# Three-layer attention and expert kernel: the first layer's maxima and subtractions taken head by head, constants and one weight load moved

## Chip, cores, metric

One core of a Trainium2 chip runs the whole kernel. The metric is the device time of the launch in microseconds (us), the median of several runs. The profiled execution is one further run whose trace was recorded.

## What is computed

The input is a batch of B = 4 sequences of S = 576 positions with 8 heads of 64 columns. Three layers follow each other; the change is in the first, a linear attention:

```python
def phi(x):
    proj = np.einsum('bhsd,df->bhsf', x, w_phi)               # 64 -> 128 features
    proj = proj - np.max(np.abs(proj), axis=-1, keepdims=True)
    return np.concatenate([np.exp(proj), np.exp(-proj)], axis=-1)
q_p, k_p = phi(q), phi(k)
kv  = np.einsum('bhsf,bhsd->bhfd', k_p, v)
z   = np.sum(k_p, axis=2)
num = np.einsum('bhsf,bhfd->bhsd', q_p, kv)
den = np.einsum('bhsf,bhf->bhs', q_p, z)[..., None] + 1e-06
x   = num / den
```

The second layer sends each position through causal attention of 2 of 4 experts, chosen by a gate on x. The third sends each position through one of 8 two-layer networks (512 to 1024 to 512 columns), with a choice that can stick to that of the position before.

## The kernel before

The first layer works on 16 units, one for each sequence and pair of heads (`PhaseA`). `raw` holds k and q of the two heads, head 0 in partitions 0 to 63 and head 1 in 64 to 127. `proj` (L221) is called three times for a unit: for k (`nm` "k", 4 tiles of 128 positions), for the last 64 positions of k and q together ("e", one tile) and for q ("q", 4 tiles). Each call multiplies by `w_phi` (L237) into one PSUM tile for each head (`pjk_0` and `pjk_1`, or `pje`, `pjq`). VectorE then takes for each head the largest absolute value of each position (L241: `mxk`, `mxe`, `mxq`) and subtracts it (L242: `uk`, `ue`, `uq`).

- `feat_k` (L245): ScalarE takes exp of +u and of -u (L251 for 512 positions of both heads in one instruction, L252 for the last 64) into the one buffer `kp`; GpSimd adds up the four tiles (L255 to L257) into `zs`.
- `feat_q` (L259): TensorE transposes `uq` of a head (L268, tile `tr`), ScalarE takes its two exps (L270, `qp`).
- `kv` (L279) multiplies v by kp into the PSUM tile `Y`; `keys` (L288) adds the column sums, and ScalarE copies Y out (L291, tile `kvt`).
- `kvtrans` (L301, L306): TensorE transposes the last columns of q (from `ue`) and the unit before's `kvt` into one PSUM tile, also called `kvt`; ScalarE copies it (L307, `kvs`).
- `num` (L323, copied into x by VectorE at L326 for one half and by ScalarE at L328 for the other) and `den` (L340, `dn` at L342, stored to DRAM as `dd` at L344) end a unit.

The order of one round is a string of step names: the projections of unit i are laid between the transpositions of unit i-1 and the products of units i-1 and i-2:

```python
A_STEPS = ("k0 e0 q0 t f0 x0 t f1 t a kv0 kv1 A t kv2 kv3 t n0 n1 z0 a t t A s0 d0 d1 t")
```

PSUM has 5 banks for the tiles `pjk`, `pjq`, `tr` and `kvt` together, given out in turn; `pje` and the tiles of `num`, `den` and the gates share two others. So the bank that a step takes in a round is fixed by how many were taken before it: in most rounds the tile of `kvtrans` (step x0) takes the bank that `pjk_0` of the same round held, and the second `tr` (step f1) that of `pjk_1`. Either can be written as soon as VectorE has subtracted that head.

A tile framework turns this into each engine's final order: it puts instructions in an order of its own, and `issue_after(ins)` tells it to issue what is recorded inside after `ins`. Before the change only the background work uses that (`Background.step`, L95; an instruction recorded with `anchor` is what it is issued after). This background work, the gate of a finished sequence, the load of the experts' weights (`wr_s`, L1099, by registers that are read from `ri_b`, L637 and L638) and their splitting in two (L1116 on ScalarE, L1117 on VectorE), runs at the steps named "t" in the later rounds. After the first two sequences are done (rounds 9 to 11) the most of it comes together with the units' own work.

`make_consts` (L143) sets up identities, a mask and a few small tables (`iota`, `lower`, `ones`) with some eight short VectorE instructions (L152 to L174, and L1011 elsewhere). `load` (L203) issues the loads of `raw`, by SyncE; for the first unit in three pieces, with the load of `w_phi` (L211) behind the first.

Of the kernel before, what the change touches and what calls it, by code (L numbers as in the profile page):

```python
# [12 lines left out]
AF = mybir.ActivationFunctionType  # L13
OP = mybir.AluOpType
AX = mybir.AxisListType
# [5 lines left out]
NF = 128  # L21
# [36 lines left out]
def rd(ap):  # L58
    return ap.bitcast(F32)
# [8 lines left out]
class Background:  # L68
# [3 lines left out]
    def __init__(self, tc):  # L72
        self.q, self.tc, self.anchors, self.now = [], tc, {}, 0

    def add(self, name, gen, held=True, lane="", after=(), at=None, wait=0, rate=1):
        e = dict(name=name, gen=gen, held=held, lane=lane, after=after, wake=self.now + wait, rate=rate)
        self.q.insert(len(self.q) if at is None else at, e)
# [67 lines left out]
def make_consts(ctx, tc, E1=4, E2=8):  # L145
    nc = tc.nc
    cp = ctx.enter_context(tc.tile_pool(name="consts", bufs=1))
    k = Consts()
    one = cp.tile([128, 128], F32, name="ones")
    make_identity(nc, one)  # L150
    eye = cp.tile([128, 128], F32R, name="ident")
    nc.vector.tensor_copy(eye, one)  # L152
    k.ident = rd(eye)
    k.identb = cp.tile([128, 128], BF16, name="identb")
    nc.vector.tensor_copy(k.identb, k.ident)
    k.mask = cp.tile([128, 128], BF16, name="cmask")
    nc.vector.memset(k.mask, 0.0)
    nc.gpsimd.affine_select(out=k.mask, in_=k.mask, pattern=[[-1, 128]], base=0, channel_multiplier=1,
                            compare_op=OP.is_ge, fill=-1e30)

    k.identr = eye[:, 0:64]
    k.maskr = cp.tile([128, 64], F32R, name="cmaskr")
    nc.vector.tensor_copy(k.maskr, k.mask[:, 0:64])
    k.ones = one
    nc.vector.memset(k.ones, 1.0)
    ii = cp.tile([128, 8], I32, name="iota_i")
    nc.gpsimd.iota(ii, pattern=[[1, 8]], base=0, channel_multiplier=0)
    k.iota = cp.tile([128, 8], F32, name="iota")
    nc.vector.tensor_copy(k.iota, ii)
    k.iota1 = cp.tile([128, 8], F32, name="iota1")  # L170
    nc.vector.tensor_scalar(k.iota1, k.iota, 1.0, None, op0=OP.add)

    k.lower = cp.tile([128, 4, 4], F32, name="lower")
    nc.vector.tensor_tensor(k.lower, k.iota[:, None, 0:4].to_broadcast([128, 4, 4]),  # L174
                            k.iota[:, 0:4, None].to_broadcast([128, 4, 4]), op=OP.is_lt)
    return k


class PhaseA:


    def __init__(self, ctx, tc, k, ps, gk, dr, hl, kq, v, w_phi, x1_tile, bg):
        nc = tc.nc
        self.gk, self.dr, self.hl = gk, dr, hl
        self.nc, self.k, self.kq, self.v, self.bg, self.x1_tile = nc, k, kq, v, bg, x1_tile
        self.p2 = ctx.enter_context(tc.tile_pool(name="a_2", bufs=2))
        self.p3 = ctx.enter_context(tc.tile_pool(name="a_3", bufs=2))
        self.p1 = ctx.enter_context(tc.tile_pool(name="a_1", bufs=2))
        self.ps = ps
        self.w_phi = self.p3.tile([128, NF], F32, name="a_w", bufs=1)  # L190
        self.w_in = w_phi
        self.vts = []
        for i in range(3):
            vt = self.p3.tile([128, QT, 2, 64], F32, name=f"a_v{i}", bufs=1)
            nc.gpsimd.memset(vt[64:128, 4], 0.0)
            self.vts.append(vt)

        self.kp = self.p3.tile([128, QT, 2, 256], F32, name="a_kp", bufs=1)
        nc.gpsimd.memset(self.kp[64:128, 4], 0.0)
        self.st = {}  # L200
        self.units = [(b, p) for b in range(B) for p in range(NP)]

    def load(self, i):  # L203

        nc, (b, p) = self.nc, self.units[i]
        raw = self.p2.tile([128, 2 * S], F32, tag="raw", name=f"raw_{i}", bufs=3)
        self.st[i] = {"raw": raw}
        for c in (slice(0, 256), slice(256, 640), slice(640, 2 * S)) if i == 0 else (slice(0, 640), slice(640, 2 * S)):
            nc.sync.dma_start(raw[:, c], self.kq[b, p, :, c])
            if i == 0 and c.start == 0:  # L210
                nc.sync.dma_start(self.w_phi, self.w_in)  # L211

    def load_v(self, i):
        nc, (b, p), r = self.nc, self.units[i], self.st[i]
# [6 lines left out]
    def proj(self, i, nm):  # L221


        nc, r = self.nc, self.st[i]
        w, raws = self.w_phi, r["raw"]
        n = 1 if nm == "e" else 4
        u = r["u" + nm] = self.p3.tile([128, n, 256], F32, tag=f"u{nm}", name=f"u{nm}_{i}")
        mx = self.p3.tile([128, 2, n], F32, tag=f"mx{nm}", name=f"mx{nm}_{i}")
        if n == 1:
            pt = [self.ps.tile([128, HALF], F32, tag="mm", name=f"pj{nm}_{i}_{h}") for h in range(2)]  # L230
        else:
            pt = [self.ps.tile([128, 512], F32, tag="X", name=f"pj{nm}_{i}_{h}") for h in range(2)]
        for t in range(n):
            for h in range(2):
                p = slice(64 * h, 64 * h + 64)
                c = dict(k=0, e=512, q=640)[nm] + 128 * t
                nc.tensor.matmul(pt[h][:, 128 * t:128 * t + 128], raws[p, c:c + 128], w[p], start=True, stop=True)  # L237
        for h in range(2):
            src = pt[h][:, 0:128 * n].rearrange("p (t f) -> p t f", f=NF)
            m = mx[:, h]  # L240
            nc.vector.tensor_reduce(m, src, axis=AX.X, op=OP.max, apply_absolute_value=True)  # L241
            self.bg.anchor(nc.vector.tensor_tensor(u[:, :, NF * h:NF * h + NF], src,  # L242
                                                   m[:, :, None].to_broadcast([128, n, NF]), op=OP.subtract))

    def feat_k(self, i):  # L245
        nc, r = self.nc, self.st[i]
        u, e = r["uk"], r["ue"]
        kp = self.kp
        zs = r["zs"] = self.p3.tile([128, 2, 2, 256], F32, tag="zs", name=f"zs_{i}", bufs=1)
        for sg, sc in ((0, 1.0), (1, -1.0)):  # L250
            nc.scalar.activation(kp[:, 0:4, sg, :], u[:, 0:4, :], AF.Exp, scale=sc)  # L251
            self.bg.anchor(nc.scalar.activation(kp[0:64, 4, sg, :], e[0:64, 0, :], AF.Exp, scale=sc))  # L252

            add = nc.gpsimd.tensor_tensor
            add(zs[:, :, sg, :], kp[:, 0:2, sg, :], kp[:, 2:4, sg, :], op=OP.add)  # L255
            add(zs[0:64, 0, sg, :], zs[0:64, 0, sg, :], kp[0:64, 4, sg, :], op=OP.add)
            add(zs[:, 0, sg, :], zs[:, 0, sg, :], zs[:, 1, sg, :], op=OP.add)  # L257
# [88 lines left out]
    def fin(self, b):  # L346
# [20 lines left out]
        for p in range(n):  # L367
            load(p)
        yield 5
        for p in range(NP):  # L370
            (nc.vector if last and p % 2 else nc.gpsimd).tensor_tensor(x1[:, p, :], x1[:, p, :], rbs[p], op=OP.mult)
            if p == 0 and n == 3:
                load(3)
            if not last:
                yield
# [1225 lines left out]
def kern(tc, kq, v, w_phi, b_gate, wqkv, wo, c_gate, w1, w2, out):  # L1601
    nc = tc.nc
    with ExitStack() as ctx:


        def pool(name, c=ctx, **kw):
            return c.enter_context(tc.tile_pool(name=name, bufs=kw.pop("bufs", 2), reuse_waits="tile", **kw))

        k = make_consts(ctx, tc)
        cp = pool("const2", bufs=1)  # L1610
        dr = ctx.enter_context(tc.tile_pool(name="dram", bufs=1, space=DRAM))
# [119 lines left out]
```

## Time and profile before

| | us |
|---|---|
| three runs | 562.77, 560.4, 562.26 |
| their median | 562.26 |
| profiled execution | 560.32 |
| its span in the trace | 558.4 |
| projections of the 16 units, first and last | start 3.2 and about 160 |

The profiled execution is 1.94 us below the median of the runs; 1.92 us of its own time lie outside its span. A page gives busy times and, in the list of costliest groups, what an engine sat idle for. A wait row names an engine and line, what it waited for, the total, the count and the longest. A timeline row gives the start, the busy time of a run of equal instructions, and in brackets the idle time before them; a chain row gives the start and the length of a piece of the chain that ended last. The program has one TensorE that is rarely idle: what matters is where it waits.

### The profile page before, as it was taken

What the parts mean: (1) busy time and instruction counts of PE and PEld (TensorE: products, weight loads), DVE (VectorE), ACT (ScalarE), POOL (GpSimd) and SP (SyncE); (2) the same over time, 40 slices, a digit from 0 to 9 for tenths busy, and PEclk for the clock granted to TensorE, in tenths of its full rate; (3) what the DMA queues carried; (4) which work ended last, traced back from release to release, by engine and by line L of the source; (5) the groups of instructions that cost most, each with busy time, mean ns of one, the idle gap of its engine ahead of it and who ended that gap; (6) DMA issues with size and microseconds to landing.
All of it is one profiled execution on the core that took longest, in us unless ns stands there. A gap on an engine that the chain in (4) does not pass through costs nothing.

```text
span 558.4 us, 11721 instructions
## 1 busy us (share of the span) xinstructions
PE 529.3 (95%) x4456; PEld 440.0 (79%) x4456; DVE 358.7 (64%) x952; ACT 269.5 (48%) x609; POOL 178.1 (32%) x222
## 2 busy tenths in 40 slices
PE   6999999899999999998998999999999999998995
PEld 5666665566667597768776888898999999997995
DVE  5776677986772777968796876842754265617450
ACT  2857465574574366947659653630442145114200
POOL 5563584368437222221103200120405040503000
PEclk9999999999999999999999999999999999999999
DMA  8323263445105222700200510273336133713011
GB/s 245 123 77 117 84 222 105 127 143 168 50 5 174 75 69 87 228 1 2 76 1 1 188 41 2 76 251 100 123 113 194 44 123 115 256 65 124 2 45 47
DMA packets 32708, 57.06 MB, mean 102 GB/s; under 512 B 7012, under 2 KB 17636, under 8 KB 31620
## 3 DMA queue, kind: packets, MB, share of 16 engines
q1 hardware_dynamic: 32644, 56.24, 31.0%
q8 instruction: 37, 0.61, 0.4%
q14 instruction: 27, 0.22, 0.1%
HBM read 41.86 MB, written 14.36 MB: 101 GB/s over the span
## 4 chain that ended last, share of the span: by engine, by line
PE 72%; DVE 14%; ACT 5%; issue 4%; DMA 4%; POOL 0%; SPq 0%; DVEq 0%; ACTq 0%; POOLq 0%
PE Y L279 6%; PE pq_s L702 6%; PE pn L323 5%; PE po_c L63 5%; PE po_c L64 5%; PE po_c L65 5%; PE ph_c L63 4%; PE ph_c L65 4%; PE ph_c L64 4%; PE py_s L848 3%; PE pd L340 3%; PE pjk L237 3%; DVE mxk L241 3%; PE pg L439 2%; PE pt_s L821 2%
## 5 line engine op out<-in xcount | busy, mean ns | idle before, releaser
L63 PE MATMUL ph_c<-xh_c,w1h_c 128*128 128x288 f32 x256 | 76.7, 300 | 0.0
L1415 ACT ACTIVATE h_c<-ph_c 128x288 fp32r<-128x288 f32 x64 | 25.8, 408 | 104.9 <-PE ph_c L65 104.6
L63 PE MATMUL po_c<-h_c,w2h_c 128*128 128x288 f32 x256 | 76.2, 297 | 0.0
L64 PE MATMUL ph_c<-xl_c,w1h_c 128*128 128x288 f32 x256 | 75.7, 296 | 0.0
L65 PE MATMUL ph_c<-xh_c,w1l_c 128*128 128x288 f32 x256 | 75.5, 296 | 0.0
L64 PE MATMUL po_c<-h_c,w2h_c 128*128 128x288 f32 x256 | 75.5, 295 | 0.0
L65 PE MATMUL po_c<-h_c,w2l_c 128*128 128x288 f32 x256 | 75.4, 295 | 0.0
L255 POOL TENSOR_TENSOR zs<-a_kp 128x512 f32<-128x512 f32 x32 | 42.3, 1336 | 68.7 <-PE Y L288 42.3
L270 ACT ACTIVATE qp<-tr 128x512 f32<-128x512 f32 x64 | 35.1, 610 | 50.2 <-PE tr L268 50.2
L1416 DVE SCALAR_TENSOR_TENSOR h_c<-ph_c,h_c 128x288 fp32r<-128x288 f32 x64 | 28.5, 453 | 33.4 <-ACT h_c L1415 33.1
L63 PEld LDWEIGHTS ph_c<-xh_c,w1h_c 128*128 128x128 f32 x256 | 48.1, 188 | 1.8 <-DVE h_c L1416 0.6
L63 PEld LDWEIGHTS po_c<-h_c,w2h_c 128*128 128x128 f32 x256 | 48.1, 188 | 0.9 <-issue 0.9
L65 PEld LDWEIGHTS ph_c<-xh_c,w1l_c 128*128 128x128 f32 x256 | 48.0, 188 | 0.5 <-issue 0.5
L1385 POOL TENSOR_TENSOR xl_c<-x,xh_c 128x576 fp32r<-128x576 f32 x16 | 26.5, 1680 | 68.4 <-ACT xh_c L1384 68.3
L64 PEld LDWEIGHTS ph_c<-xl_c,w1h_c 128*128 128x128 f32 x256 | 48.1, 188 | 0.0
L65 PEld LDWEIGHTS po_c<-h_c,w2l_c 128*128 128x128 f32 x256 | 48.1, 188 | 0.0
L64 PEld LDWEIGHTS po_c<-h_c,w2h_c 128*128 128x128 f32 x256 | 48.1, 188 | 0.0
L702 PE MATMUL pq_s<-xh_b,w_s 128*128 128x288 f32 x192 | 43.6, 305 | 2.7 <-DVE q_s L670 1.7
L1437 DVE TENSOR_TENSOR fo_c<-po_c,pb 128x288 f32<-128x288 f32 x32 | 14.4, 455 | 47.7 <-PE po_c L65 29.6
L279 PE MATMUL Y<-a_kp,a_v 128*64 128x256 f32 x320 | 41.1, 386 | 0.0
L251 ACT ACTIVATE a_kp<-uk 128x1024 f32<-128x1024 f32 x32 | 33.6, 1052 | 13.0 <-DVE uk L242 6.4
L1370 POOL TENSOR_TENSOR w2l_c<-w2raw_c,w2h_c 128x1024 fp32r<-128x1024 f32 x6 | 17.4, 2921 | 65.6 <-ACT w2h_c L1368 65.6
(314 smaller groups left out, 1268.4 us busy)
## 6 DMA issues: line engine op xcount, KB each, us to landing
w1raw_c<-in_w_dram SPq DMA_DIRECT2D x16, 512.0 KB, 4.3
w2raw_c<-in_w_dram SPq DMA_DIRECT2D x16, 512.0 KB, 5.0
raw<-in_kq_dram SPq DMA_DIRECT2D x15, 320.0 KB, 3.1
rb<-d SPq DMA_DIRECT2D x32, 144.0 KB, 3.5
x1d<-x SPq DMA_DIRECT2D x4, 1152.0 KB
x2d<-x SPq DMA_DIRECT2D x4, 1152.0 KB
raw<-in_kq_dram SPq DMA_DIRECT2D x16, 256.0 KB, 3.5
a_v<-in_v_dram SPq DMA_DIRECT2D x16, 256.0 KB, 4.2
```

The lines of the kernel that those rows point to most:

```text
L63: nc.tensor.matmul(out, lh, rh, start=start, stop=False, **kw)
L64: nc.tensor.matmul(out, lh, rl, start=False, stop=False, **kw)
L65: return nc.tensor.matmul(out, ll, rh, start=False, stop=stop, **kw)
L251: nc.scalar.activation(kp[:, 0:4, sg, :], u[:, 0:4, :], AF.Exp, scale=sc)
L255: add(zs[:, :, sg, :], kp[:, 0:2, sg, :], kp[:, 2:4, sg, :], op=OP.add)
L270: self.bg.anchor(nc.scalar.activation(qp[:, h, sg, 0:512], tp, AF.Exp, scale=sc))
L279: nc.tensor.matmul(Y[64 * h:64 * h + 64, 0:256], vt[:, t, h, :], kp[:, t, :, h * NF:(h + 1) * NF], start=t == 0, stop=t == 4)
L323: nc.tensor.matmul(pn[64 * h:64 * h + 64, :], kvs[:, sg, 64 * h:64 * h + 64], qp[:, h, sg, c], start=sg == 0, stop=sg == 1)
L702: self.nc.tensor.matmul(out, self.wqkv[t][:, wj, ch, 0:m], x[:, ch, c], start=wj == ch == 0 and x is xh, stop=wj == 1 and ch == 3)
L1385: self.bg.anchor(nc.gpsimd.tensor_tensor(xl[:, ch], x[:, ch], rd(xh[:, ch]), op=OP.subtract))
L1415: nc.scalar.activation(hh[:, c], ph, AF.Relu),
L1416: nc.vector.scalar_tensor_tensor(hl[:, c], ph, 0.0, rd(hh[:, c]), op0=OP.max, op1=OP.subtract))
```

## The change

In `proj`, each reduction is issued after `self.last`, which is at first the last of the constants (`k.last`, the instruction that makes `lower`) and from then on the latest subtraction of k. In the first unit, ScalarE takes the exps of k head by head (four of 512 columns in place of two of 1024). The load of `w_phi` is issued by ScalarE, no longer by SyncE. In the changed kernel the lines below move by one or by twelve: L241 is L244, L242 is L245, L251 is L263 (in the first unit L260), L268 is L280, L326 is L338.

```diff
--- before.py
+++ after.py
@@ -171,8 +171,8 @@
     nc.vector.tensor_scalar(k.iota1, k.iota, 1.0, None, op0=OP.add)
 
     k.lower = cp.tile([128, 4, 4], F32, name="lower")
-    nc.vector.tensor_tensor(k.lower, k.iota[:, None, 0:4].to_broadcast([128, 4, 4]),
-                            k.iota[:, 0:4, None].to_broadcast([128, 4, 4]), op=OP.is_lt)
+    k.last = nc.vector.tensor_tensor(k.lower, k.iota[:, None, 0:4].to_broadcast([128, 4, 4]),
+                                     k.iota[:, 0:4, None].to_broadcast([128, 4, 4]), op=OP.is_lt)
     return k
 
 
@@ -197,6 +197,7 @@
 
         self.kp = self.p3.tile([128, QT, 2, 256], F32, name="a_kp", bufs=1)
         nc.gpsimd.memset(self.kp[64:128, 4], 0.0)
+        self.last = k.last
         self.st = {}
         self.units = [(b, p) for b in range(B) for p in range(NP)]
 
@@ -208,7 +209,7 @@
         for c in (slice(0, 256), slice(256, 640), slice(640, 2 * S)) if i == 0 else (slice(0, 640), slice(640, 2 * S)):
             nc.sync.dma_start(raw[:, c], self.kq[b, p, :, c])
             if i == 0 and c.start == 0:
-                nc.sync.dma_start(self.w_phi, self.w_in)
+                nc.scalar.dma_start(self.w_phi, self.w_in)
 
     def load_v(self, i):
         nc, (b, p), r = self.nc, self.units[i], self.st[i]
@@ -238,17 +239,28 @@
         for h in range(2):
             src = pt[h][:, 0:128 * n].rearrange("p (t f) -> p t f", f=NF)
             m = mx[:, h]
-            nc.vector.tensor_reduce(m, src, axis=AX.X, op=OP.max, apply_absolute_value=True)
-            self.bg.anchor(nc.vector.tensor_tensor(u[:, :, NF * h:NF * h + NF], src,
-                                                   m[:, :, None].to_broadcast([128, n, NF]), op=OP.subtract))
+            with ExitStack() as c:
+                c.enter_context(self.bg.tc.issue_after(self.last.ins))
+                nc.vector.tensor_reduce(m, src, axis=AX.X, op=OP.max, apply_absolute_value=True)
+            last = nc.vector.tensor_tensor(u[:, :, NF * h:NF * h + NF], src,
+                                           m[:, :, None].to_broadcast([128, n, NF]), op=OP.subtract)
+            if nm == "k":
+                self.last = last
+            self.bg.anchor(last)
 
     def feat_k(self, i):
         nc, r = self.nc, self.st[i]
         u, e = r["uk"], r["ue"]
         kp = self.kp
         zs = r["zs"] = self.p3.tile([128, 2, 2, 256], F32, tag="zs", name=f"zs_{i}", bufs=1)
+        if not i:
+            for h in range(2):
+                for sg, sc in ((0, 1.0), (1, -1.0)):
+                    c = slice(h * NF, (h + 1) * NF)
+                    nc.scalar.activation(kp[:, 0:4, sg, c], u[:, 0:4, c], AF.Exp, scale=sc)
         for sg, sc in ((0, 1.0), (1, -1.0)):
-            nc.scalar.activation(kp[:, 0:4, sg, :], u[:, 0:4, :], AF.Exp, scale=sc)
+            if i:
+                nc.scalar.activation(kp[:, 0:4, sg, :], u[:, 0:4, :], AF.Exp, scale=sc)
             self.bg.anchor(nc.scalar.activation(kp[0:64, 4, sg, :], e[0:64, 0, :], AF.Exp, scale=sc))
 
             add = nc.gpsimd.tensor_tensor
```

VectorE at the start of the program, before, from its third instruction on (uk, ue: the subtracted k and last columns of unit 0; `_0` and `_1` behind pjk and pje are the heads):

```order
L241 TENSOR_REDUCE mxk_159<-pjk_0_160 128x4
L241 TENSOR_REDUCE mxk_159<-pjk_1_161 128x4
L242 TENSOR_TENSOR uk_158<-pjk_0_160,mxk_159 128x4x128
L242 TENSOR_TENSOR uk_158<-pjk_1_161,mxk_159 128x4x128
L169 CAST iota<-iota_i 128x8
L241 TENSOR_REDUCE mxe_175<-pje_0_176 128x1
L152 CAST ident<-ones 128x128
L163 CAST cmaskr<-cmask 128x64
L171 TENSOR_SCALAR iota_79<-iota 128x8
L155 CAST identb<-ident 128x128
L165 MEMSET ones 128x128
L174 TENSOR_TENSOR lower<-iota 128x16
```

And with the change:

```order
L169 CAST iota<-iota_i 128x8
L152 CAST ident<-ones 128x128
L163 CAST cmaskr<-cmask 128x64
L171 TENSOR_SCALAR iota_79<-iota 128x8
L155 CAST identb<-ident 128x128
L165 MEMSET ones 128x128
L174 TENSOR_TENSOR lower<-iota 128x16
L1023 COPY b_ex<-iota 128x8
L244 TENSOR_REDUCE mxk_159<-pjk_0_160 128x4
L245 TENSOR_TENSOR uk_158<-pjk_0_160,mxk_159 128x4x128
L244 TENSOR_REDUCE mxk_159<-pjk_1_161 128x4
L245 TENSOR_TENSOR uk_158<-pjk_1_161,mxk_159 128x4x128
```

The constants now stand in front of the first reduction, and each head of k is reduced and subtracted before the other is begun.

VectorE in unit 3, whose k is `pjk_0_429` and `pjk_1_430` before:

```order
L326 COPY x_0_391<-pn_1_399 128x288
L241 TENSOR_REDUCE mxk_428<-pjk_0_429 128x4
L241 TENSOR_REDUCE mxk_428<-pjk_1_430 128x4
L242 TENSOR_TENSOR uk_427<-pjk_0_429,mxk_428 128x4x128
L242 TENSOR_TENSOR uk_427<-pjk_1_430,mxk_428 128x4x128
L241 TENSOR_REDUCE mxe_444<-pje_0_445 128x1
```

And with the change, where the same tiles are `pjk_0_431` and `pjk_1_432`:

```order
L338 COPY x_0_393<-pn_1_401 128x288
L244 TENSOR_REDUCE mxk_430<-pjk_0_431 128x4
L245 TENSOR_TENSOR uk_429<-pjk_0_431,mxk_430 128x4x128
L244 TENSOR_REDUCE mxk_430<-pjk_1_432 128x4
L245 TENSOR_TENSOR uk_429<-pjk_1_432,mxk_430 128x4x128
L244 TENSOR_REDUCE mxe_446<-pje_0_447 128x1
```

Only the second and third row of k have changed places; it is so in every unit from 3 to 9 and from 12 to 15.

VectorE in round 10, where the second half of the gate of the first two sequences runs (`perm`, `ws`, `ri_b`: the experts chosen; `x_1`: a half of unit 7's result; `dn`: its denominators; `uk_1418`: k of unit 10), before:

```order
L468 TENSOR_REDUCE perm_0_1377<-u_0_1342 128x4
L520 TENSOR_REDUCE ws_1381<-c_0_1379 128x20
L637 CAST ri_b_0_1383<-perm_0_1377 1x1
L637 CAST ri_b_1_1395<-perm_0_1377 1x1
L326 COPY x_1_900<-pn_1_1325 128x288
L342 TENSOR_SCALAR dn_1354<-pd_0_1355 128x288
L342 TENSOR_SCALAR dn_1354<-pd_1_1365 128x288
L241 TENSOR_REDUCE mxk_1419<-pjk_0_1420 128x4
L241 TENSOR_REDUCE mxk_1419<-pjk_1_1421 128x4
L242 TENSOR_TENSOR uk_1418<-pjk_0_1420,mxk_1419 128x4x128
L242 TENSOR_TENSOR uk_1418<-pjk_1_1421,mxk_1419 128x4x128
```

And with the change (the reduction of k's first head, `mxk_1421<-pjk_0_1422`, stands nine rows before the first of these, its subtraction five rows before):

```order
L338 COPY x_1_902<-pn_1_1327 128x288
L472 TENSOR_REDUCE rk_1346<-u_0_1344 128x4
L245 TENSOR_TENSOR uk_1420<-pjk_1_1423,mxk_1421 128x4x128
L475 TENSOR_TENSOR hot_0_1348<-rk_1346,iota 128x16
L354 TENSOR_SCALAR dn_1356<-pd_0_1357 128x288
L478 TENSOR_TENSOR u_0_1344<-hot_0_1348,iota 128x16
L529 TENSOR_TENSOR c_0_1381<-w_0_1213,hot_0_1348 128x80
L480 TENSOR_REDUCE perm_0_1379<-u_0_1344 128x4
L532 TENSOR_REDUCE ws_1383<-c_0_1381 128x20
L354 TENSOR_SCALAR dn_1356<-pd_1_1367 128x288
L649 CAST ri_b_0_1385<-perm_0_1379 1x1
L649 CAST ri_b_1_1397<-perm_0_1379 1x1
```

Unit 10's k, which stood behind the gate and both `dn`, is now mixed with the gate's last steps; the two `ri_b` stood in front of `x_1` and both `dn` and now stand behind them.

SyncE at the same place (`wsd`, `dd`: stores of the gate and of `dn`; `wr_s`: the first weights of the second layer), before:

```order
L1026 DMA wsd<-ws_1381 128x20
L638 TENSOR_LOAD ri_b_0_1383
L638 ISA x2
L638 TENSOR_LOAD ri_b_1_1395
L638 ISA x2
L1099 ISA
L1099 DMA wr_s_1407<-in_wqkv_dram 128x768
L1099 ISA
L1099 DMA wr_s_1407<-in_wqkv_dram 128x768
L344 DMA dd_901<-dn_1354 4x576
```

And with the change:

```order
L1038 DMA wsd<-ws_1383 128x20
L356 DMA dd_903<-dn_1356 4x576
L650 TENSOR_LOAD ri_b_0_1385
L650 ISA x2
L650 TENSOR_LOAD ri_b_1_1397
L650 ISA x2
L1111 ISA
L1111 DMA wr_s_1409<-in_wqkv_dram 128x768
L1111 ISA
L1111 DMA wr_s_1409<-in_wqkv_dram 128x768
```

The store `dd` stood behind the weights and now stands in front of the register loads that the weights' addresses come from.

## Rows read from the trace of the kernel before

**Rows 1.** Part 1 of the page: busy us, share of the span, instructions.
```profile
PE 529.3 (95%) x4456; PEld 440.0 (79%) x4456; DVE 358.7 (64%) x952; ACT 269.5 (48%) x609; POOL 178.1 (32%) x222
```

**Rows 2.** Waits of PE, stretch 0 to 210.
```profile
PE kvt L301 <- DVE uk L242: 4.6, 11, 1.0
...
PE tr L268 <- DVE uk L242: 0.4, 1, 0.4
```

**Rows 3.** Timeline of PE in round 5, 46.7 to 51.3.
```profile
49.95 0.41 PE L301 MATMUL kvt<-ident,ue 128*128 128x128 f32 x2 [0.36 <-DVE uk L242]
...
50.55 0.63 PE L268 MATMUL tr<-ident,uq 128*128 128x128 f32 x4
```

**Rows 4.** Timeline of DVE, the same stretch.
```profile
47.92 1.29 DVE L241 TENSOR_REDUCE mxk<-pjk 128x4 f32<-128x512 f32 x2 [0.97 <-PE pjk L237]
49.12 1.28 DVE L242 TENSOR_TENSOR uk<-pjk,mxk 128x512 f32<-128x512 f32 x2
```

**Rows 5.** Chain of waits, 46.8 to 50.6, between uk and kvt: start, length, piece.
```profile
49.82 0.14 issue
```

**Rows 6.** Timeline of DVE, unit 9: a head's subtraction right behind its own reduction.
```profile
95.54 0.68 DVE L241 TENSOR_REDUCE mxq<-pjq 128x4 f32<-128x512 f32 x1
96.25 0.69 DVE L242 TENSOR_TENSOR uq<-pjq,mxq 128x512 f32<-128x512 f32 x1
```

**Rows 7.** Chain of waits at the start, 0 to 18.
```profile
1.17 0.42 SPq L211
...
5.89 1.27 DVE mxk L241 x2
...
8.36 0.08 DVE iota L169
8.44 0.19 DVE mxe L241
...
9.31 0.20 DVE ue L242
...
9.65 0.46 PE pje L237 x2
```

**Rows 8.** Timeline of DVE and ACT, 8 to 21: unit 2's first reduction, ScalarE's copy of Y.
```profile
18.12 0.69 DVE L241 TENSOR_REDUCE mxk<-pjk 128x4 f32<-128x512 f32 x1 [0.85 <-PE pjk L237]
...
19.20 0.47 ACT L291 ACTIVATE kvt<-Y 128x384 f32<-128x384 f32 x1
```

**Rows 9.** Timeline of PE, round 2: kvt and the second tr.
```profile
20.15 0.41 PE L301 MATMUL kvt<-ident,ue 128*128 128x128 f32 x2
...
21.82 0.66 PE L268 MATMUL tr<-ident,uq 128*128 128x128 f32 x4
```

**Rows 10.** Timeline of PE, rounds 10 and 11, 97 to 119.6.
```profile
103.93 1.18 PE L340 MATMUL pd<-qp,kvs 128*32 128x288 f32 x16 [0.65 <-DVE x L326]
...
108.19 0.63 PE L268 MATMUL tr<-ident,uq 128*128 128x128 f32 x4
...
115.74 0.37 PE L237 MATMUL pje<-a_w,raw 64*128 64x128 f32 x1 [0.56 <-DVE x L326]
...
118.97 0.41 PE L301 MATMUL kvt<-ident,ue 128*128 128x128 f32 x2 [0.48 <-DVE uk L242]
```

**Rows 11.** Timeline of DVE, SP and ACT around the weights of the second layer.
```profile
103.32 0.19 DVE L637 CAST ri_b<-perm 1x1 int32<-1x1 f32 x2
...
105.18 0.46 DVE L342 TENSOR_SCALAR dn<-pd 128x288 f32<-128x288 f32 x1 [0.94 <-PE pd L340]
...
105.48 0.90 SPq L1099 DMA_DIRECT2D wr_s<-in_wqkv_dram  x2
...
111.44 1.20 ACT L1116 ACTIVATE w_s<-wr_s 128x512 fp32r<-128x512 f32 x2
112.48 0.46 ACT L328 ACTIVATE x<-pn 128x288 f32<-128x288 f32 x1
```

**Rows 12.** The tile wr_s: its loads, time to landing.
```profile
DMA to landing us min/median/max: 2.9/2.9/3.2
```

## Prediction

> **What bounds the kernel now.** I read the page's busy times first. TensorE is busy 95% of the span [rows 1], so the time changes only where it waits. The list of TensorE's waits for the first layer comes next [rows 2]: the most frequent is that of kvt's transposition for the subtraction of k, 11 times, 4.6 us in all, and once more at the first tr (unit 13, 0.4). In a timeline of one round [rows 3] it shows as a pair: TensorE stands idle until kvt can start at 49.95, does kvt, and starts the second tr at 50.55. VectorE's rows beside it [rows 4] say what both wait for: two reductions from 47.92, two subtractions from 49.12, so that the first one ends at 49.81 and the second at 50.40. kvt follows the first end by 0.14, which the chain calls issue [rows 5], and tr follows the second by 0.15. Both starts of a round are thus set by VectorE's four instructions. I then read the start, rounds 9 to 11 and the weights behind them, where the order changes most.
>
> **Steady rounds: a loss.** No instruction is added or taken away in them; the second reduction and the first subtraction change places. Independent neighbours start 0.60 apart: two reductions take 1.29 together, and the first subtraction starts 1.20 behind the first reduction [rows 4]. A subtraction right behind the reduction that it needs starts 0.71 later [rows 6], 0.11 more. Before, no neighbours of k depended on each other; with the change two pairs do. The second subtraction ends 0.71 + 0.60 + 0.71 + 0.68 = 2.70 behind the first reduction's start, before 1.20 + 1.28 = 2.48: +0.22. The first subtraction ends 0.49 earlier, so kvt comes earlier; but the second tr stands right behind it on TensorE and goes when the second subtraction is done, so the 0.49 becomes a wait at tr in place of the one at kvt. The bound above: the subtraction has in most rounds a second wait, on ScalarE, which could stand as an instruction of its own in front of it; the nearest row for the cost of a wait that is released is the 0.14 of [rows 5], of which 0.03 is already in the 0.71, so 0.33 in all. I take 0.27, the middle, since neither row is of this very case. It holds in units 3 to 9 and 12 to 15, which is 11 units (of the wait row's 11 counts one is unit 11, below, and unit 13 is the count at tr [rows 2]): **+3.0**, ends +2.4 and +3.6. The Trainium skill, "VectorE: DVE Perf Modes", section "The DRAIN you can't avoid", speaks against this term: the next VectorE instruction doesn't begin before the one ahead has left the pipe, and a semaphore between them costs nothing extra. By that rule the term is 0 and the sum below is 3.0 lower; this trace doesn't agree, with 0.71 against 0.60 for the same shapes.
>
> **The start: a gain.** Four edits act on one path. (1) SyncE's issue of `w_phi` is 0.42 [rows 7], and 0.05 lies beside it; on ScalarE's queue it frees the next piece of `raw` by that much, and the first reduction moves from 5.89 to about 5.5. ScalarE's own first work comes much later, so the issue costs nothing there. (2) The constants between the subtraction of k and that of e take 9.31 - 8.36 - 0.19 (the reduction among them) = 0.76 [rows 7]; ahead of the first reduction VectorE has nothing else to do until 5.5, so they cost nothing there. (3) The dependent pairs give 0.22 per unit back. (4) The exps of head 0 can start while VectorE is at head 1; four short ones for two long ones, on an engine that then waits for e anyway, priced at nothing (were it not so, Y of unit 0 would be late by less than one 0.6 piece, which end below covers). From 5.5 on VectorE is the chain: a unit is eight long instructions at 0.60, four short ones at 0.20 (8.44 to 8.63 is one) and the two gaps of 0.11, 5.82 us. So unit 2's first reduction starts at 5.5 + 2 x 5.82 = 17.1, before 18.12 [rows 8]. Its subtraction no longer stands behind one of q and ends at 17.1 + 0.71 + 0.68 = 18.5, which frees kvt at 18.65, before 20.15 [rows 9]: 1.5 earlier. The second subtraction ends at 17.1 + 2.70 = 19.8, which frees the second tr at 19.95, before 21.82: 1.9 earlier, if nothing else is late. What is late next is ScalarE's copy of Y, at 19.20 [rows 8], which kvt's second half needs, behind the exps of tr. I take **-1.5**, kvt's number; ends -1.9 (VectorE alone) and -0.4 (only the earlier piece of `raw` comes through).
>
> **Rounds 9 to 11.** Unit 9 is in the steady term. In round 10 unit 10's k is mixed with the gate's last steps, and the copy x stands behind one and a half heads of k. The second `pd`, which waits 0.65 for that copy [rows 10], waits some tenths longer; but k is then done, and what follows `pd` (e, q, the transpositions) no longer waits behind four instructions of VectorE. By the instruction times the two come out within 0.1 at the second tr (108.19 before): **0**. In round 11 the copy of x, for which pje waits 0.56, and k, for which kvt waits 0.48 [rows 10], come nearer: at most 1.0 is to be had. I take half of it, **-0.5**. The other end, +1.2, is the length of the two ScalarE casts of the weights [rows 11], if they come to stand in front of that copy's chain. SyncE's moves cost nothing in themselves: the store dd goes past the register loads, and what that can do is rival C. Behind round 12 the order is the same as before.
>
> **Sum:** +3.0 - 1.5 + 0 - 0.5 = +1.0 us. The profiled execution took 560.32 and would take 561.3. The median of the runs shown, 562.26, is 1.94 above it; I forecast the median, **563.3**. Some 0.5% (2.8 us) is what a measurement of this kernel can tell from no change: the three runs alone spread by 2.4.
>
> **Rivals.**
> A is the forecast: 563.3; with its terms half-way to their ends, 562.3 to 564.6. Chance 0.50.
> B: a dependent pair costs no more than an independent one, and the steady term is 0. For it: the extra 0.11 is small and could belong to the place where it was read. Against it: it is there for the same two shapes [rows 6]. Sum -2.0, 560.3. Chance 0.10. The rule of the Trainium skill named above is this case.
> D: the start gives all that VectorE's own chain gives (-1.9), round 11 the whole of its waits (-1.0), and the loss is at its lower end (+2.4): -0.5, 561.8. For it: after the start TensorE's bank waits are all on VectorE, and little else is seen late. Against it: ScalarE's copy at 19.20 [rows 8] has no slack to spare. Chance 0.22.
> C, slower: the second layer's weights come late. Before, the two `ri_b`, from which SyncE reads the weights' addresses, were written at 103.32, and the weights were issued 2.2 later at 105.48 [rows 11]. With the change they stand behind the second `dn`, which starts at 105.18 [rows 11] and sooner in no case that I see, and SyncE has dd's store to issue first: the `ri_b` come at about 105.9, the issue at some 108.5 to 108.9, the landing 2.9 later [rows 12] at 111.4 to 111.8. ScalarE casts them at 111.44 [rows 11], now behind a 1.1 exp of k, so at about 112.5, and that still fits. It decides the time if they land after about 113.3: then the copies of x behind the casts, and so pje, wait. A landing 2 us late costs 2.0 and the 0.5 of round 11: +3.5, 565.8. Chance 0.14.
> That the change doesn't do what it says is excluded: the new order has reduction, subtraction, reduction, subtraction of k in all 16 units. The remaining 0.04 is for what I don't see, three parts of four slower.
>
> **Range and chances.** 560.4 to 566.2. Below it lies half of B; above it the worse part of C and all three terms of A at their bad ends (3.6 - 0.4 + 1.2 = +4.4): together about 0.15. Faster by over 0.5% needs B with start and middle at their good ends (-1.9 - 1.0 = -2.9): half of B and a little, 0.06. Slower by over 0.5%: C, and the slower part of the unseen, 0.17. The same: 0.77.
>
> **What would show it.** Right: in steady rounds kvt without a wait and a wait of TensorE at the second tr, for uk's line, with the subtraction of a head 0.71 behind its reduction and tr some 2.85 behind the first reduction's start (2.63 before); unit 2's kvt near 18.7 and its second tr before 20.6; round 10's second tr within 0.3 of 108.2 plus what the rounds before lost; weights landing before 113. Wrong: a second subtraction that still ends 2.5 behind (B), a wait of ScalarE for wr_s of more than a few tenths (C), or a unit 2 that starts its kvt no earlier than 19.7. If the steady rounds lose 0.3 each and the time still falls, the gain at the start was priced too low.

## The result and the profile after

The changed kernel takes 566.67 us (median of 5 runs, 564.72 to 567.51) and the kernel before 562.53 in runs beside it: ratio 1.0078, 95% interval 1.0054 to 1.0103. It is slower by 4.1 us, 0.8%. The forecast said 563.3, +1.0 us, and "the same"; the measured time lies 0.5 above the range. The profiled execution took 567.51 (span 565.7) and is the slowest of the five.

Busy times and the granted clock by slices, from the page of the changed kernel (to be held against [rows 1]):

```profile
PE 532.2 (94%) x4456; PEld 442.0 (78%) x4456; DVE 361.2 (64%) x952; ACT 270.2 (48%) x611; POOL 177.5 (31%) x222
...
PEclk9999999989999999999999999999999999999999
```

The work is the same; the span is longer, so there is more waiting. The ninth slice (113 to 127) has a lower clock, which the kernel before did not have there. TensorE's waits in 0 to 210, for [rows 2]:

```profile
PE tr L280 <- DVE uk L245: 5.9, 10, 0.6
...
PE pje L238 <- ACT x L340: 1.3, 1, 1.3
PE pc L512 <- DVE cnt L509: 1.2, 2, 0.9
PE pjq L238 <- DMA raw<-in_kq_dram: 0.8, 1, 0.8
PE kvt L313 <- DVE uk L245: 0.7, 1, 0.7
...
PE pje L238 <- DVE x L338: 0.4, 1, 0.4
```

The wait at kvt (4.6 us, 11 times) has become a wait at tr (5.9 us, 10 times). In round 11 pje waits 1.7 in all where it waited 0.6, and at the start the projection of q waits for its load.

**A steady round.** Round 5 again, TensorE (for [rows 3]), then VectorE (for [rows 4]), then the chain between the first reduction and the first subtraction (start, length, piece):

```profile
51.41 0.41 PE L313 MATMUL kvt<-ident,ue 128*128 128x128 f32 x2
51.65 0.49 PE L318 MATMUL kvt<-ident,kvt 128*128 128x128 f32 x3
52.73 0.63 PE L280 MATMUL tr<-ident,uq 128*128 128x128 f32 x4 [0.58 <-DVE uk L245]
```

```profile
49.77 0.69 DVE L244 TENSOR_REDUCE mxk<-pjk 128x4 f32<-128x512 f32 x1 [0.97 <-PE pjk L238]
50.57 0.69 DVE L245 TENSOR_TENSOR uk<-pjk,mxk 128x512 f32<-128x512 f32 x1
51.18 0.68 DVE L244 TENSOR_REDUCE mxk<-pjk 128x4 f32<-128x512 f32 x1
51.89 0.69 DVE L245 TENSOR_TENSOR uk<-pjk,mxk 128x512 f32<-128x512 f32 x1
```

```profile
50.48 0.03 issue
50.50 0.02 DVEq L245
50.52 0.04 issue
```

The second pair is 0.71 apart, as forecast. The first is 0.80 apart: a wait instruction of its own (DVEq) stands in front of the subtraction that also waits for ScalarE. So tr goes 2.96 behind the first reduction (52.73 - 49.77), where it went 2.63 behind it: +0.33 in such a round. kvt no longer waits, and TensorE stands idle 0.58 right behind it.

**Where the time goes.** The table follows the start of a unit's projection of k in the profiled executions (us from the span's start), for the two kernels and for second executions of them, `b_again` and `c_again`:

| | unit 3 | units 3 to 9 | units 9 to 15 |
|---|---|---|---|
| before | 26.58 | 63.10 | 69.25 |
| before, second execution | 26.20 | 63.10 | 69.26 |
| change | 27.78 | 65.04 | 71.20 |
| change, second execution | 26.37 | 65.04 | 71.47 |

Six steady units cost 1.94, to 0.01 the same in both executions: 0.32 a unit. Units 9 to 15 cost 2.0 and 2.2 against these two executions of the kernel before, of which steady units make 1.2; others with the order of before took 0.8 longer there (both below). The start is 1.2 later in one execution and 0.2 earlier in the other, against the first execution of the kernel before. Behind unit 15 the order is the same; single executions still differ by 1 to 2 us there, those of the kernel before among themselves too (spans 558.4 and 560.5), so single spans settle nothing and the medians do.

### The profile page after: what moved, and what is told of

The parts are those of the page before. It is cut to its first block, busy times and chain, and to the rows that moved or that the text cites. A ratio compares the mean times of both kernels' runs of the same rounds, so it can differ in the third digit from the quotient of the medians.

```text
span 565.7 us, 11725 instructions
## 1 busy us (share of the span) xinstructions
PE 532.2 (94%) x4456; PEld 442.0 (78%) x4456; DVE 361.2 (64%) x952; ACT 270.2 (48%) x611; POOL 177.5 (31%) x222
## 4 chain that ended last, share of the span: by engine, by line
PE 72%; DVE 14%; ACT 5%; DMA 5%; issue 2%; SPq 1%; POOL 0%; DVEq 0%; ACTq 0%; POOLq 0%
PE Y L291 6%; PE pq_s L714 6%; PE ph_c L63 5%; PE ph_c L65 5%; PE ph_c L64 5%; PE po_c L63 5%; PE po_c L64 5%; PE po_c L65 5%; PE pn L335 5%; DVE uk L245 3%; PE py_s L860 3%; DVE mxk L244 3%; PE pd L352 3%; PE pjk L238 3%; PE pg L451 2%
## 5 line engine op out<-in xcount | busy, mean ns | idle before, releaser
L267 POOL TENSOR_TENSOR zs<-a_kp 128x512 f32<-128x512 f32 x32 | 41.0, 1296 | 73.1 <-PE Y L300 52.3
L263 ACT ACTIVATE a_kp<-uk 128x1024 f32<-128x1024 f32 x30 | 31.5, 1051 | 9.7 <-issue 6.8
```

## Experiments

Theory S: the order by heads costs the steady rounds 0.33 each, and the late weights of round 11 add to it. Its rival R: the loss comes from the start and from loads that happen to land late. For the start, theory W (moving `w_phi` makes q's load late) stood against V (load times differ from one execution to the next). The kernel before, run beside them, had medians of 562.03 (first four), 562.21 (next four) and 561.47 (last four).

**e1_unit0: the order by heads in unit 0 alone.**

```diff
-            if nm == "k":
+            if nm == "k" and i == 0:
                 self.last = last
```

> The change with its order by heads kept in unit 0 alone; constants first, the first exps by head and w_phi by ScalarE stay. Theory S (the steady rounds lose 0.33 each by the order of k, 11 units, and rounds 10 and 11 lose 0.6 more together): about 3.6 to 4.2 us are given back, so 562.5 to 563.1 against 566.7 for the change, and TensorE's wait is at kvt again, about 0.36 a round. Rival R (the loss is in the start and in chance landings of DMAs): no more than 1 us comes back, 565.7 or above.

562.17, ratio 1.001 (0.999 to 1.003). 4.5 us came back, a little over S's upper figure, and the wait is at kvt again. TensorE's waits for k's subtraction in 20 to 95, seven rounds of e1_unit0 (the kernel before has the same row there):

```profile
PE kvt L313 <- DVE uk L245: 3.2, 7, 1.0
```

R is out: the start's edits were all still there but the order by heads in units 1 and 2, which e7 keeps.

**e2_wphi: the kernel before with `w_phi` by ScalarE.**

```diff
-                nc.sync.dma_start(self.w_phi, self.w_in)
+                nc.scalar.dma_start(self.w_phi, self.w_in)
```

> The kernel before with w_phi issued by ScalarE and nothing else. Theory W (moving w_phi makes the loads of the first unit share the DMA engines in another way: the first matmul starts at 3.46 and not 3.17, q's piece lands at 6.8 and not 5.2, and TensorE then stays longer at the slow matmuls of the start): the third unit is 0.5 to 1.5 us later than before, 563.0 to 564.0. Rival V (landings differ from execution to execution and this one was a late one): within 0.5 of before, 562.0 to 563.0, or a little faster.

561.01, ratio 0.9976 (0.9958 to 0.9994): 1.0 us faster, not slower, by an interval that just leaves 1 out, and q's projection waits for nothing. W is out as it was put.

**e3_wphi_back: the change with `w_phi` by SyncE.**

```diff
-                nc.scalar.dma_start(self.w_phi, self.w_in)
+                nc.sync.dma_start(self.w_phi, self.w_in)
```

> The change with w_phi issued by SyncE again. Theory W: the start gives 1.5 to 2 us back, 564.7 to 565.2, with q's piece landing before 5.5. Rival V: the time of the change, 566.2 to 567.2.

566.21, ratio 1.0072 (1.0047 to 1.0097), which the change's interval covers. Its start was 1.85 earlier than that of the change (unit 3 at 25.93), as W said, but the median did not follow. So the late start of the change's first profile was not what its runs have in common.

**e4_not_9_11: the change without the order by heads in units 9 to 11.**

```diff
-            if nm == "k":
+            if nm == "k" and i not in (9, 10, 11):
```

> The change with the order by heads left out in units 9 to 11. Theory S with late weights (the weights' landing and a drop of TensorE's clock behind it cost 2.2 in round 11, round 10 gives 0.9 back, unit 9 costs 0.33): 1.0 to 1.7 us less than the change, 565.0 to 565.7, no wait of pje above 0.6 in round 11 and a granted clock of 1.00 there. Rival: round 10's gain and round 11's loss cancel, 566.2 to 567.0.

565.70, ratio 1.0064 (1.0042 to 1.0086): 1.0 less than the change, at the low edge of what S said; the intervals overlap. The profile is clearer. Units 9 to 15 take 70.08, 0.83 over the kernel before, which is units 12 to 14 alone; the weights are not late, and pje waits 0.56 as before:

```profile
117.87 0.37 PE L238 MATMUL pje<-a_w,raw 64*128 64x128 f32 x1 [0.56 <-DVE x L338]
```

So the steady order costs 6 x 0.32 (units 3 to 8) + 0.33 (9) + 0.83 (12 to 14) + 0.33 (15) = 3.4 us; for units 9 and 15 the 0.33 of round 5 is put in, they were not measured alone. Of units 9 to 15's loss, 1.16 (units 9 and 12 to 14) is steady, and the rest, +0.8 and +1.1 in the two executions of the change, is rounds 10 and 11. In e3 and e10, with the same order there, that rest is -0.2 and +0.1; what sets the four executions apart is TensorE's clock (see the part on rounds 10 and 11).

**e5_fill_tr: the change, with the first matmuls of Y in front of the second tr.**

```diff
-A_STEPS = ("k0 e0 q0 t f0 x0 t f1 t a kv0 kv1 A t kv2 kv3 t n0 n1 z0 a t t A s0 d0 d1 t")
+A_STEPS = ("k0 e0 q0 t f0 x0 t kv0 f1 t a kv1 A t kv2 kv3 t n0 n1 z0 a t t A s0 d0 d1 t")
```

> The change with the first eight matmuls of Y (step kv0) put between kvt and the second tr in every round. Theory S (all that the order by heads costs in a steady round is TensorE idle at the second tr, 0.58 to 0.62 in 11 rounds): the idle time is filled, 5.5 to 6.5 us less than the change, 560.2 to 561.2, with no wait of tr for uk. Rival (Y's inputs, kp or the free bank Y, come no earlier, so the wait moves to Y): 565.5 to 567.

564.70, ratio 1.0045 (1.0030 to 1.0061): 2.0 less than the change, not 6. In the steady rounds S is right: no wait for uk is left in 20 to 95, and units 3 to 9 take 62.20, 2.8 less than in the change and 0.9 less than before. The profile, of the slowest of its twelve runs (566.79), loses most of it again around rounds 10 and 11, where TensorE stands idle for the gate and its clock falls (columns: stretch, length, busy us and counts of PE, PEld, DVE, ACT, POOL, then the granted clock, DMA share, GB/s):

```profile
96.00:100.00 4.00, 2.29 (x32) 1.49 (x28) 3.86 (x9) 4.00 (x8) 2.36 (x3) 1.00 0.29 80
100.00:104.00 4.00, 3.05 (x18) 1.54 (x18) 3.87 (x13) 0.84 (x2) 3.06 (x4) 0.78 0.00 0
```

**e6_fill_kvt: the kernel before with `w_phi` by ScalarE and the first matmuls of Y in front of kvt.**

```diff
-A_STEPS = ("k0 e0 q0 t f0 x0 t f1 t a kv0 kv1 A t kv2 kv3 t n0 n1 z0 a t t A s0 d0 d1 t")
+A_STEPS = ("k0 e0 q0 t f0 kv0 x0 t f1 t a kv1 A t kv2 kv3 t n0 n1 z0 a t t A s0 d0 d1 t")
```

> The kernel before with w_phi by ScalarE and the first eight matmuls of Y put between the first tr and kvt. Theory S: the 0.36 that TensorE waits for the first subtraction in 11 rounds (4.5 us in all) is filled, and with nothing lost elsewhere it takes 557.0 to 558.0 (the kernel with w_phi alone took 561.0). Rival (the later second tr makes ScalarE's exps and with them num or the next Y late): 560.5 to 562.

558.94, ratio 0.9936 (0.9910 to 0.9962): **faster than both kernels**, by 3.3 and 7.7 us, though 1 to 2 short of what was expected. Units 3 to 9 take 60.58, 2.5 less than before, without any wait for uk; units 9 to 15 take 66.78, again 2.5 less. Of the 3.3 us, 1.0 came with `w_phi` alone (e2, 561.01), so that the place of Y is worth some 2.1 by the medians. The profiled execution, 556.64, is the third fastest of ten. The longest wait left in it is the gate of round 10, which VectorE reaches no earlier (1.4 before); that it keeps the median from more was not tested:

```profile
PE pc L500 <- DVE cnt L497: 3.1, 1, 3.1
```

**e7_units0_2: the order by heads in units 0 to 2 alone.**

```diff
-            if nm == "k":
+            if nm == "k" and i < 3:
```

> The change with the order by heads kept in units 0 to 2 alone: the start of the change as it is, the steady rounds and rounds 9 to 11 as before. If the start loses 1.2 as its profile shows (TensorE's slow matmuls last to 10.0 there, to 6.3 before): 563.2 to 564. If that was one execution's load times and the start usually gives 0.3 to 0.6: 561.0 to 562.0.

561.99, ratio 0.9999 (0.9979 to 1.0018). The start of this program is that of the change, instruction for instruction, and in this execution unit 3 stood at 25.62, 2.2 earlier than in the change's first profile. So V: the start differs by execution, and over runs all its edits together are worth nothing that can be measured, to within 1.2 us.

**e8_cast_late: the change with the splitting of the weights begun later.**

```diff
-                    bg.add("cast_" + slots[0].nm, pb.cast_w(slots[0]), lane="w")
+                    bg.add("cast_" + slots[0].nm, pb.cast_w(slots[0]), lane="w", wait=12)
```

> The change with the splitting of the first weights (L1128, L1129) begun twelve background steps later, nothing else. Theory C (the weights land late, ScalarE waits for them in front of its copy of x, and pje behind that): the wait of pje in round 11 goes from 1.3 + 0.4 to under 0.6, TensorE's clock stays at 1.00 there, and 1.3 to 2.2 us come back: 564.5 to 565.4. Rival (round 11 is late because k stands in another place on VectorE): 566.2 to 567, with the waits of pje where they are.

564.91, ratio 1.0049 (1.0025 to 1.0072): 1.8 less than the change, as C said. The waits of pje are gone, but not all came back. TensorE, the timeline of e8_cast_late in rounds 11 and 12:

```profile
117.18 0.41 PE L313 MATMUL kvt<-ident,ue 128*128 128x128 f32 x2 [1.10 <-DVE uk L245]
...
126.20 1.18 PE L352 MATMUL pd<-qp,kvs 128*32 128x288 f32 x16 [1.50 <-DVE x L338]
```

The casts now meet round 12, and the copy of x behind them is late there.

**c_again and b_again: both kernels once more.**

> The changed kernel once more, nothing else, for its start and its round 11. If the start differs from one execution to the next (theory V): q's piece may land in time, the slow matmuls then end before 7.5 and unit 3 starts 0.3 to 1.0 earlier than before instead of 1.2 later. If the start of the change is always late (theory W): q waits again by 0.5 or more, unit 3 1.0 to 1.4 later. Round 11 in both: pje waits 1.3 to 2.0 in all.

> The kernel before once more, nothing else. Theory V: its own start can be late as well, unit 3 within 0 to +1.5 of the first profile. Theory W (only with w_phi on ScalarE's queue does q's piece come late): unit 3 within 0.3 of the first profile, slow matmuls to about 6.3.

565.91 and 562.31, one run each. The starts are in the table: the change at 26.37, before at 26.20. W is out for the change: q did not wait and unit 3 was 0.2 earlier than in the kernel before. That is V's direction, but short of its figures (0.3 to 1.0 earlier, slow matmuls to 7.5; they lasted to 7.9). The waits of pje, 1.9, are as expected. For the kernel before, unit 3 came 0.38 earlier than in its first profile, which neither theory had covered, and W's slow matmuls "to about 6.3" lasted to 9.0, with no wait of TensorE among them.

**e9_q_late: the kernel before, with q's piece issued behind unit 1's loads.**

```diff
-        for c in (slice(0, 256), slice(256, 640), slice(640, 2 * S)) if i == 0 else (slice(0, 640), slice(640, 2 * S)):
+        for c in (slice(0, 256), slice(256, 640)) if i == 0 else (slice(0, 640), slice(640, 2 * S)):
...
         self.load(1)
+        b, p = self.units[0]
+        self.nc.sync.dma_start(self.st[0]["raw"][:, 640:2 * S], self.kq[b, p, :, 640:2 * S])
```

> The kernel before with the third piece of unit 0 (q) issued behind both pieces of unit 1, nothing else. If a wait of TensorE at about 6 us is what prolongs its slow matmuls: it waits for q by 0.8 or more and the matmuls stay slow to beyond 9, as in the change. If the slow stretch has a fixed length: it ends at about 6.3 to 7.2 and only the wait itself is lost.

563.75, one run. q waits 0.72, and the matmuls (417 ns each while slow, 272 in the median later) stay slow to 12.45:

```profile
7.17 2.08 PE L237 MATMUL pjq<-a_w,raw 64*128 64x128 f32 x16 [0.72 <-DMA raw<-in_kq_dram]
9.04 1.92 PE L237 MATMUL pjk<-a_w,raw 64*128 64x128 f32 x16
...
11.38 1.93 PE L237 MATMUL pjq<-a_w,raw 64*128 64x128 f32 x15
```

The stretch is not of fixed length, and here it was longer behind a wait; b_again shows that it can be long without one.

**e10_unit1_later: the change with the loads of unit 1 behind v of unit 0.**

```diff
         self.load(0)
-        self.load(1)
         self.load_v(0)
+        self.load(1)
```

> The change with the loads of unit 1 issued behind v of unit 0. If q's piece is late because unit 1's pieces share the DMA engines with it: q lands before 5.7, slow matmuls end before 7.5, unit 3 starts at least 0.5 before the kernel before, and the median comes 0.5 to 1.5 below the change, 565.2 to 566.2. If not: as the change, 566.2 to 567.

566.22, ratio 1.0107 (1.0050 to 1.0164): no gain. The slow matmuls end at 7.1, as was expected if the loads share, but unit 3 stands at 26.35, as in c_again, and not 0.5 before the kernel before.

## Why the prediction was wrong

By its own steps, with what the runs showed in their place:

| term | forecast | its ends | measured |
|---|---|---|---|
| steady, 11 units | +3.0 | +2.4 to +3.6 | +3.4 |
| start | -1.5 | -1.9 to -0.4 | 0.0, from -0.8 to +1.4 |
| rounds 10 and 11 | 0 and -0.5 | to -1.0 and +1.2 | -0.2 to +0.3 at equal clock (+0.8 and +1.1 with a fall, against none) |

The start is unit 3 in six executions of the change's start (27.78, 26.37, 26.76, 25.62, 25.76, 26.35: mean 26.44) against two of the kernel before (mean 26.39). By the profiles that is 3.4 + 0 + 0 = 3.4; the medians say 4.1, with an interval of 3.0 to 5.8. In the last of the six, e10, unit 1's loads stand elsewhere.

**Steady: right in mechanism, 0.4 too small.** The wait moved from kvt to the second tr, and the early kvt brought nothing. The 0.27 a unit was the middle of two ends; the wait instruction in front of the subtraction makes it the upper one, 0.33, in most units. Rival B is out: 0.71 and 0.80 here between dependent neighbours, 0.60 between independent ones. So the rule of the Trainium skill, "VectorE: DVE Perf Modes", section "The DRAIN you can't avoid", that a semaphore between two VectorE instructions costs nothing extra, does not hold for these pairs. The same section also says that a next instruction that is not held starts earlier, which the forecast left out and which fits the 0.60.

**The start is the step that failed.** The forecast took "-1.5, kvt's number" and left ScalarE's copy of Y, "late next", to the ends. The chain of c_again, 0 to 28, shows the two parts:

```profile
5.56 0.68 DVE mxk L244
...
14.90 1.21 DVE mxq L244 x2
...
19.64 0.38 ACT kvt L303
20.02 0.04 issue
20.06 1.08 PE Y L291 x6
21.14 0.37 PE kvt L313 x2
...
26.44 1.14 PE pjk L238 x16
```

To 16.1 it is VectorE, as forecast, with the first reduction at 5.56 (forecast 5.5) and the constants gone from between. Unit 2's first subtraction was done at 19.00 (forecast 18.5). But TensorE did not take kvt then: in the new order six matmuls of Y stand in front of it, and they wait for ScalarE's copy, which ends at 20.02. Before, it ended at 19.67. The copy was therefore no earlier at all, and all that VectorE had gained ended there: kvt went at 21.07 and the second tr at 21.68 (forecast 18.65 and 19.95; before 20.15 and 21.82). The other executions of this start bear it out: the copy starts between 18.79 and 20.95, Y waits 0.34 for it in each, and unit 3 starts 6.83 or 6.84 behind it in all six. The forecast had read the order for VectorE and not for what stands in front of kvt on TensorE. Its other end, -1.9 at the second tr, had the same gap: in the kernel before, too, six matmuls of Y stood in front of that tr, which did not wait for VectorE.

The second thing it could not know from one execution: the first matmuls. In the change's first profile,

```profile
3.46 2.08 PE L238 MATMUL pjk<-a_w,raw 64*128 64x128 f32 x16 [3.46 <-DMA raw<-in_kq_dram]
...
6.81 2.08 PE L238 MATMUL pjq<-a_w,raw 64*128 64x128 f32 x16 [0.84 <-DMA raw<-in_kq_dram]
8.68 1.99 PE L238 MATMUL pjk<-a_w,raw 64*128 64x128 f32 x13
```

they are slow to 10.0, in the kernel before's to 6.3, in others to 6.2, 7.9 or 9.1. The page prints full speed there in all of them, but that is no reading: the trace's record of the granted clock starts only at 10.22 in the change, 6.71 in the kernel before, 8.12 in c_again, 9.32 in b_again and 12.79 in e9_q_late, each time where the slow matmuls end. In c_again the same matmuls are as slow once more, from 117.35 to 120.76, where the record has 0.50 (the second row has the columns of e5):

```profile
117.88 2.12 PE L238 MATMUL pjq<-a_w,raw 64*128 64x128 f32 x15
```

```profile
118.00:120.00 2.00, 2.00 (x19) 1.78 (x16) 1.97 (x4) 0.00 (x0) 1.92 (x2) 0.50 0.06 9
```

So by their length, 417 in both places, the first matmuls run at the lower of TensorE's two levels (1.2 GHz). Why that stretch differs in length stays open; e9 shows only that it can be long behind a wait. In the six executions of the change's start, unit 3 is the later the later it ends (6.2, 6.8, 7.1, 7.9, 9.1, 10.0 give 25.62 to 27.78 in that order); in the two of the kernel before it is not (6.3 and 9.0 give 26.58 and 26.20). The Trainium skill, "TensorE: Matmul & The Clock Gate", section "What's actually happening", states that the number of slow matmuls at a kernel's start differs from run to run; these executions agree (7.9 and 10.0 for the change, 6.3 and 9.0 for the kernel before).

**Rounds 10 and 11: rival C's wait came, but no clear loss with it.** SyncE, ScalarE, VectorE and TensorE of the change, from their timelines (for [rows 10, 11]):

```profile
108.25 0.54 SPq L356 DMA_DIRECT2D dd<-dn  x1
110.82 0.90 SPq L1111 DMA_DIRECT2D wr_s<-in_wqkv_dram  x2
```

```profile
116.20 1.15 ACT L1128 ACTIVATE w_s<-wr_s 128x512 fp32r<-128x512 f32 x2 [1.58 <-DMA wr_s<-in_wqkv_dram]
117.26 0.39 ACT L340 ACTIVATE x<-pn 128x288 f32<-128x288 f32 x1
```

```profile
118.08 0.45 DVE L338 COPY x<-pn 128x288 f32<-128x288 f32 x1
```

```profile
117.70 0.49 PE L238 MATMUL pje<-a_w,raw 64*128 64x128 f32 x2 [1.30 <-ACT x L340]
118.58 0.37 PE L238 MATMUL pje<-a_w,raw 64*128 64x128 f32 x1 [0.39 <-DVE x L338]
```

The program is 1.9 to 2.3 us late here, so the weights' issue at 110.82 is the 108.5 to 108.9 that C gave. The cast that waits for them starts 5.4 behind the first issue (116.20 - 110.82), and 4.2 behind it in c_again (113.59 - 109.39); the forecast had put 2.9 [rows 12], which is the time of one load, and there are two, the second issued 0.56 behind the first. The trace has no landing of these two, and why they took longer is not shown. ScalarE waited 1.58, with its own copy of x and VectorE's behind it. What C had not got: round 10 gains more than the "0" forecast, because unit 9's and 10's k no longer stand behind the gate (in c_again the shift against the kernel before falls from 1.74 at unit 9 to 0.47 at unit 11), and round 11 loses 2.4 again (to 2.91 at the pd of round 12), not 2.0 on top of nothing. It need not even wait for the weights by much: in c_again that wait is 0.39, and VectorE's part of the splitting is slow instead.

Two things make round 11's loss larger in some executions. VectorE's subtraction for the weights (L1129) can fall just behind GpSimd's add, and then it waits; c_again, VectorE and GpSimd:

```profile
114.26 2.81 DVE L1129 TENSOR_TENSOR w_s<-wr_s,w_s 128x512 fp32r<-128x512 f32 x2 [1.06 <-ACT w_s L1128]
```

```profile
114.09 1.30 POOL L267 TENSOR_TENSOR zs<-a_kp 128x512 f32<-128x512 f32 x1 [8.95 <-PE Y L300]
```

The two took 1.28 in the kernel before, where they began at 114.03 and the add of GpSimd, which the trace has from 114.02, was the one to be long:

```profile
114.02 2.46 POOL L255 TENSOR_TENSOR zs<-a_kp 128x512 f32<-128x512 f32 x1 [10.27 <-ACT a_kp L251]
...
114.03 1.28 DVE L1117 TENSOR_TENSOR w_s<-wr_s,w_s 128x512 fp32r<-128x512 f32 x2
```

In c_again the add was 0.17 ahead and kept its 1.30; the subtractions took 2.81, which is 1.5 us for the copy of x and the pje behind it. The Trainium skill, "SBUF — State Buffer", section "SBUF: two separate sides", has a rule for it: of a VectorE instruction with two SBUF inputs and a GpSimd one, the first to start holds the port pair that they share, and the other waits. c_again agrees. For the kernel before the record has the add 0.02 ahead as well, and yet the add was the one to wait; so small a lead of GpSimd's in the trace decides nothing. In the first execution of the change the add was done by 116.82 and the two took 1.29 at 116.87. And TensorE's clock falls after its idle time; the change (columns as in e5):

```profile
116.00:118.00 2.00, 0.70 (x10) 0.51 (x6) 1.13 (x2) 1.79 (x5) 0.81 (x1) 1.00 0.95 277
118.00:120.00 2.00, 1.61 (x20) 1.42 (x18) 1.97 (x5) 2.00 (x4) 1.82 (x3) 0.86 0.42 118
120.00:122.00 2.00, 2.00 (x10) 1.78 (x10) 2.00 (x3) 0.70 (x3) 1.92 (x2) 0.50 0.02 7
```

TensorE was busy 0.70 of 2.00, and then runs at 0.50, the lower of its two levels (1.2 GHz). e3 and e10 have waits of pje like the change's, 2.0 us, and a clock of 1.00 throughout, and their rounds 10 and 11 come out 0.7 to 1.3 us better.

Such a fall also comes without the change. With the order of before in rounds 9 to 14, it came at the gate of round 10 in three of six executions; e1_unit0, then the kernel before:

```profile
100.00:104.00 4.00, 4.00 (x32) 1.79 (x32) 3.35 (x13) 0.98 (x2) 3.00 (x4) 0.63 0.02 3
```

```profile
100.00:104.00 4.00, 3.35 (x37) 1.55 (x40) 3.93 (x17) 1.32 (x3) 3.51 (x5) 1.00 0.00 0
```

Units 9 to 15 took 70.04, 70.00 and 70.04 with it (e1, e2, e9) and 69.25, 69.26 and 69.25 without (before, b_again, e7): 0.8 us for the fall. With the change's order they took 71.20 and 71.47 with a fall in round 11 and 70.20 and 70.51 without (e3, e10). Compared at equal clock, and less the 1.16 of the steady units, rounds 10 and 11 of the change cost 0.0 and +0.3, or -0.2 and +0.1: round 10's gain and round 11's loss about cancel, and the -0.5 forecast did not come. The lower medians of e4 and e8 leave room for a loss of some tenths that these profiles do not show; their intervals overlap with the change's.

The chances: the outcome was given 0.17. All three terms came out worse than forecast, by 0.4, 1.5 and 0.5, where the range had set good ends of some against bad ends of others. That makes 2.4 of the 3.1 us between +1.0 and +4.1; the other 0.7 lies within the interval of the measurement and is not explained.

## What to carry to other kernels

Where two steps of the bottleneck engine wait for two results of another engine, finishing the first result earlier pays only if work stands between the two; otherwise the later end decides, and the dependent order makes that one later. Fill the gap with independent work of the bottleneck engine (here Y in front of kvt, some 2.1 us) before reordering the producer. A gain on a helper's chain is worth what the next input of the waiting instruction allows: read the new order on the waiting engine, in front of that instruction, and on every engine whose result stands there.

## What was not expected of the hardware

The first matmuls of the program take 417 ns against 272 later, for a time that differs between executions of one and the same kernel (to 7.9 in c_again, 10.0 in the change). The page prints a granted clock of 1.00 there, though the trace has a record of it only from where the slow matmuls end (8.12 and 10.22); matmuls of the same shape take 417 again where the record has 0.50. A VectorE subtraction of 128x512 took 0.68 us alone and 2.81 for two where GpSimd's add had begun 0.17 ahead of it.
